# A filter with products of 128 columns, a re-ordered list, and the second gate/up tile in one piece

## The chip, the cores and the metric

One core of a Trainium2 chip runs the kernel. The metric is the device time of one execution in microseconds (us). The engines are TensorE (PE in the profile, with its weight loads apart as PEld), VectorE (DVE), ScalarE (ACT), GpSimd (POOL) and SyncE (SP, which issues most DMAs).

## The reference

Sequence S = 2048, width D = 512, hidden width F = 1376, all float32, one batch:

```python
def _A_ref(x, w_r, w_i):                      # spectral filter
    X = jnp.fft.rfft2(x, axes=(-2, -1))
    X = X * (w_r + 1j * w_i)                  # (2048, 257)
    return jnp.fft.irfft2(X, s=(S, D), axes=(-2, -1))

def _B_ref(x, w_gate, w_up, w_down):          # GEGLU
    h = _gelu(x @ w_gate) * (x @ w_up)        # tanh form of gelu
    return h @ w_down

h  = x + _A_ref(_layernorm(x), w_r, w_i)
h2 = h + _B_ref(_layernorm(h), w_gate, w_up, w_down)
```

## The kernel before

Both Fourier transforms are matmuls with cosine and sine tables. The kernel runs through these stages, each behind the other on TensorE:

- **START** (0 to 30 us): layer norm, and the transform over the sequence while x is loaded.
- **SECOND** (30 to 74 us), the filter, 16 blocks t of 128 rows of the spectrum. `over_d(t)` (step o; L423) transforms over D into two banks of PSUM, ScalarE copies them out as `dp` (L427, two copies of 64 partitions). `filtered(t)` (step f; L434) finishes the transform over the sequence from `dp`; DVE multiplies with the filter's weights `wt` (L440 to L442), and POOL adds the two products as `z` (L450, then L451, a correction of one column; for the last block DVE does this, with a part on POOL, L448). `back(t)` (step b; L461) begins the inverse. Step p patches two columns of `wt`, and each step h splits one piece of a gate or up weight into a high and a low part (ACT L156, POOL L157). `o` writes the banks that it names, in turn two pairs; a block's product therefore waits until ScalarE has copied out the block that had these banks before it.
- **FIRST** (74 to 119.5 us): the inverse over D (U, L527) and over the sequence (M, L866), the residual, the second layer norm, then, for pairs of row blocks, normalized blocks (R, ACT L909), their transposes (T, L560 and L566), and sums and differences of these, since gate, up and down are done by a scheme with 7 products in place of 8. Each operand is split into a high part (ACT) and a low part (DVE or POOL, L588), as each product is three float32r matmuls (`mm3`, L163 to L165). Steps a to o of a pair are these copies, sums and splits; K (POOL L827 to L830) prepares further row blocks; wl splits the down weights (POOL L508). The seven products P0 to P6 of the first gate/up tiles, g0 and g1, run between the steps, each tile in two halves a and b of 256 columns.
- Then tiles g2 and on, with the down products (L766), in a written order, 512 columns at a time, to the end, where `end` adds the last sums and stores them (L1211, L1216, L1217), the last block in two halves of 256 columns.

START, SECOND and FIRST are strings of step names. Inside them every engine runs its instructions in the order of the string, waiting in place for what an instruction needs. So the order of the work around the change is what these lists say: an engine can't pass an instruction of its own that waits.

In the filter one bank holds two parts of NQ/2 = 130 columns (even and odd frequencies; 129 and 128 are used, the rest are zeros of the tables). So L423 gives 4 products of 130 columns a block, `dp` has 520 columns and L434 gives 2 products of 260.

Of the kernel before, what the change touches and what calls it, by code (L numbers as in the profile page):

```python
# [19 lines left out]
S, D, F = 2048, 512, 1376  # L20
P = 128
# [3 lines left out]
NQ = 260  # L25
# [21 lines left out]
ROOTS = {0: 1, 1: 1, 2: 2, 4: 4, 8: 4, 12: 4}  # L47

FIRST = """
u0.1 u4.0 w4 C4.0 V4.2 X4 w0 C0.1 V0.3 X0 U1.2 C1.4 V1.0 X1 r0 U5.3 C5.5 V5.1 M4.1 O4.0 M0.2 O0.1 U2.3 H4 H0 X5 C2.5  # L50
V2.3 M5.1 H5 I4 G4 O5.0 G0 I0 S4 S0 A4 A0 E0.5 U7.2 C7.1 M1.3 O1.1 g0awh H1 Q0 N0 U6.0 C6.0 V7.4 X2 U3.4 C3.5 I5 G5 S5
M2.1 V6.3 R00 I1 G1 S1 A5 A1 R01 U9.7 C9 H2 X7 V3.1 X3 T00 a0 Q1 T01.2 s0.0 O2.1 U8.4 C8 E1.6 N1 R11 M7.0 c0 d0 f0
U12.3 e0.1 k0 R10 H7 b0 O7.0 g0 h0 C12 X6 M6.4 H6 i0 j0 T11.1 s1.2 r1 l0 T10 c1 d1 G2 I2 M3.2 O3.1 H3 G7 a1 b1 I7 S7
O6.0 U15.3 C15 e1.0 f1 g1 U14.5 C14 U10.4 C10 m0 k1 n1 g0aP0 g0ac1 g1aP0 l1 g0aP3 g0aP1 G3 I3 S3 A7 A3 Q3 g0aP2 I6 n0
G6 h1 g1ac1 E3.7 N3 g1aP2 i1 R31 T31.5 g1aP1 o1 R30 T30 S2 S6 A6 A2 g1ac2 j1 E2.6 Q2 N2 o0 g1aP4 g0awl s3.6 c3 g0ac2
g0aP4 R20 T20 a3 g1ac3 g1aP5 d3 e3.4 K9.5 m1 g0ad1 g0ac3 g0aP5 f3 b3 h3 g0ady g0aP6 i3 j3 R21 T21.7 g3 g1aP3 a2 b2
g0bP0 g0bP1 g1bP0 K12.4 g1ad1 g1ady g1aP6 r2 l3 k3 s2.8 g1aG0 c2 d2 f2 e2.7 k2 g1bP1 g1am0 g0bc1 g2 g0bP2 g1bc1 r3 n3
n2 o3 g1bP2 g0ad2 o2 g0aG0 g0am0 l2 m2 m3 g0bP3 h2 K8.4 g0aG1 g0am1 g0bc2 g0bP4 g1bd1 i2 j2 g1bc2 g1bP4 g1bG0 g1ad2
g0bc3 g0bd1 g0bdy g0ai0 g0ao0 g1aG1 g1bP3 g1ai0 g1am1 g1bc3 g1bdy g0ai1 g0ao1 g0bP6 g0bd2 g1awh g1awl g1ai1 g0bG1
g0bP5 hc g1bP6 lo1 lo2 g0bG0 g0bm0 g0bi0 g1bP5 g1bm0 g1bi0 g1bd2 g1bG1 g0bo0 U13.7 C13 lo3 g0bm1 g0bi1 U11.6 C11 g1bm1  # L60
g1bi1 g1ao0 g0bo1 g1bo0 g1bo1 g1ao1 g2P0
"""
# [57 lines left out]
def kernel(  # L120
# [48 lines left out]
    ps = ctx.enter_context(tc.tile_pool(name="ps", bufs=1, space=PSUM)).tile([P, 8, 512], F32, name="ps")  # L169
# [7 lines left out]
    k3 = ctx.enter_context(tc.tile_pool(name="k3", bufs=1))  # L177
# [57 lines left out]
    with (  # L235
# [146 lines left out]
        def keep_half(b):  # L382
            return dve.tensor_copy(*kept_of(b, slice(0, 2)))

        steps = {
            "s": stats,
            "g": merge,
            "m": mean,
# [21 lines left out]

        w1s.close()
        w2 = ctx2.enter_context(tc.tile_pool(name="w2", bufs=2, reuse_waits="tile"))
        dps, zs = {}, {}

        def over_d(t, k):

            pd = ps[:, k : k + 2]  # L420
            for c, (e, q) in enumerate(((0, 0), (1, 1), (0, 1), (1, 0))):
                o = pd[:, e, q * NQ // 2 : (q + 1) * NQ // 2]
                pe.matmul(o, ts[:, t, c].rearrange("p x b k -> p (x b k)"), dfs[:, c], start=True, stop=True)  # L423
            pdv = pd[:, :, :NQ].rearrange("p e (s q) -> p s e q", s=2)
            dps[t] = w2.tile([P, 2, 2, NQ // 2], F32, name="dp", bufs=5)
            for h, d in ((slice(0, 64), 1), (slice(64, P), -1)):
                act.activation(dps[t][h], pdv[h, ::d], AF.Copy)  # L427

        def filtered(t):
            dp, wt = dps.pop(t), wts.pop(t)  # L430
            px = ps[:, 4 + 2 * (t % 2) : 6 + 2 * (t % 2), :NQ]
            for g in range(2):
                r = dp[:, g].rearrange("p e q -> p (e q)")
                pe.matmul(px[:, g], cfs[:, min(t, 1), g], r, start=True, stop=True)  # L434
# [5 lines left out]
            dve.tensor_tensor(t1, px, wt[:, 0], op=ALU.mult)  # L440
# [9 lines left out]
            eng.tensor_tensor(z[:, :, first], t1[:, :, first], t2[:, :, first], op=ALU.add)  # L450
            eng.tensor_tensor(z[:, :, 0], z[:, :, 0], z[:, :, 128], op=ALU.add)  # L451
# [19 lines left out]
        with tc.manual_schedule(engines={et.PE, et.Activation, et.DVE, et.Pool}):  # L471
# [452 lines left out]
    def half(n, h):

        for k, f in tile_of(n, slice(2 * h, 2 * h + 2)).items():
            do[f"g{n}{'ab'[h]}{k}"] = f
        if not h:
# [62 lines left out]
    def second_half():  # L991
# [212 lines left out]
        def end(c, r, k, onto=False, halves=1, by=dve):  # L1204

            w = wds[NF - 1]
            for h in range(halves):
                cols = slice(h * 512 // halves, (h + 1) * 512 // halves)
                o = ps[:, k + h, : 512 // halves]
                for hw, ha in ((0, 0), (0, 1), (1, 0)):  # L1210
                    pe.matmul(o, w[:, hw, c * P : (c + 1) * P], last_a[:, ha, r, cols], start=not onto and hw + ha == 0, stop=hw == 1, skip_group_check=True)  # L1211
# [4 lines left out]
                by.tensor_tensor(to, o, to, op=ALU.add)  # L1216
                nc.sync.dma_start(ot[:, r, c, cols], to)  # L1217
# [89 lines left out]
def _tables():  # L1307
# [119 lines left out]
```

## Time and profile before

| what | value |
|---|---|
| time, median of 3 runs | 440.44 us (440.41 to 441.14) |
| the profiled execution | 440.5 us, its span 438.6 us |
| TensorE busy | 432.0 us, 98% of the span, 2275 matmuls recorded |
| DVE, ACT, POOL busy | 314.2, 243.1, 314.5 us |
| DMA | 41.61 MB, mean 95 GB/s |

In the tables of the profile a row of a timeline gives the start and the length in us (a run of like instructions is one row), the engine, the line, the operation, output <- inputs, the tiles' sizes and how often; brackets at the end give idle time of the engine just ahead and what ended it. A matmul of float32 is recorded as two. The length of a matmul row has its drain in it, so the pace of TensorE is read from the distance of starts.

### The profile page before, as it was taken

The page shows a single profiled execution, that of the slowest core. Times are in us where ns is not written, and L with a number is a line of the kernel's source. Part 1 is how long each engine was busy: PE and PEld are TensorE (multiplying, and loading weights), DVE is VectorE, ACT ScalarE, POOL GpSimd, SP SyncE. Part 2 cuts the span into 40 slices and gives each one's busy share as a digit, 9 for nine tenths or more (in the row PEclk, how much of TensorE's full clock was granted, in tenths as well). Part 3 has the DMA queues.
Part 4 walks back from the last instruction along what each step waited for, and adds up shares of the span by engine and source line. Part 5 has one row for each costly group of instructions (what it writes and reads, how often), then busy time and mean ns, then how long its engine had stood idle before and what let it go on. Part 6 is the DMA issues. An engine that isn't in the chain of part 4 may idle for free.

```text
span 438.6 us, 6625 instructions
## 1 busy us (share of the span) xinstructions
PE 432.0 (98%) x2275; PEld 366.8 (84%) x2275; DVE 314.2 (72%) x576; ACT 243.1 (55%) x502; POOL 314.5 (72%) x346
## 2 busy tenths in 40 slices
PE   8999999999999999999999999999999999999996
PEld 8999999789978777877888888888888888888885
DVE  5968896897864766368734579578677787687785
ACT  5989785799712442124432787376455653565640
POOL 6987796999859788648653944067879779787821
PEclk9999999999999999999999999999999999999999
DMA  8996904320023112112220203501212021200005
GB/s 284 400 411 85 380 10 156 128 73 24 25 96 97 49 53 92 48 50 72 72 73 24 72 25 120 169 11 62 73 48 72 28 69 49 72 24 2 0 2 192
DMA packets 23542, 41.61 MB, mean 95 GB/s; under 512 B 4178, under 2 KB 9810, under 8 KB 23380
## 3 DMA queue, kind: packets, MB, share of 16 engines
q1 hardware_dynamic: 23364, 41.05, 27.9%
q8 instruction: 18, 0.29, 0.3%
q10 hardware_dynamic: 144, 0.13, 0.1%
q14 instruction: 16, 0.13, 0.1%
HBM read 36.97 MB, written 4.20 MB: 94 GB/s over the span
## 4 chain that ended last, share of the span: by engine, by line
PE 80%; POOL 8%; DMA 5%; ACT 3%; issue 2%; DVE 1%; SPq 0%; DVEq 0%; POOLq 0%
PE ps L163 15%; PE ps L164 15%; PE ps L165 15%; PE ps L766 14%; PE ps L1105 11%; DMA gh<-in_x 3%; PE ps L527 3%; POOL z L450 3%; PE ps L866 2%; ACT dp L427 2%; DMA raw<-in_wgu 1%; PE ps L974 1%; POOL gu L157 1%; POOL pn L339 1%; PE ps L1211 1%
## 5 line engine op out<-in xcount | busy, mean ns | idle before, releaser
L163 PE MATMUL ps<-cb,gu 128*128 128x512 f32 (+1 forms) x336 | 127.2, 378 | 0.3 <-DVE a L692 0.3
L165 PE MATMUL ps<-cb,gu 128*128 128x512 f32 (+1 forms) x336 | 124.9, 372 | 0.0
L164 PE MATMUL ps<-cb,gu 128*128 128x512 f32 (+1 forms) x336 | 124.9, 372 | 0.0
L670 ACT ACTIVATE s<-ps 128x512 f32<-128x512 f32 (+1 forms) x72 | 40.4, 562 | 87.1 <-PE ps L165 86.7
L228 POOL TENSOR_TENSOR gu<-raw,gu 128x768 fp32r<-128x768 f32 (+1 forms) x42 | 61.3, 1481 | 29.0 <-DVE gu L223 16.7
L163 PEld LDWEIGHTS ps<-cb,gu 128*128 128x128 f32 x336 | 63.3, 188 | 12.3 <-issue 1.0
L164 PEld LDWEIGHTS ps<-cb,gu 128*128 128x128 f32 x336 | 63.3, 188 | 11.6 <-issue 1.0
L165 PEld LDWEIGHTS ps<-cb,gu 128*128 128x128 f32 x336 | 63.3, 188 | 11.1
L766 PE MATMUL ps<-wd,a 128*128 128x512 f32 x264 | 63.6, 393 | 0.0
L766 PEld LDWEIGHTS ps<-wd,a 128*128 128x128 f32 x264 | 49.1, 188 | 11.6 <-DVE gh L975 1.0
L679 DVE TENSOR_TENSOR ps<-ps,s 128x512 f32<-128x512 f32 (+1 forms) x48 | 31.1, 651 | 28.1 <-PE ps L165 25.3
L1112 DVE TENSOR_TENSOR gh<-ps,gh 128x512 f32<-128x512 f32 x66 | 44.2, 681 | 0.8 <-PE ps L1105 0.8
L676 ACT ACTIVATE s<-s 128x512 f32<-128x512 f32 (+1 forms) x48 | 28.4, 593 | 20.8 <-DVE s L673 20.7
L673 DVE TENSOR_TENSOR s<-ps,s 128x512 f32<-128x512 f32 (+1 forms) x48 | 30.7, 641 | 5.8 <-PE ps L165 4.7
L772 DVE TENSOR_TENSOR gh<-ps,gh 128x512 f32<-128x512 f32 x24 | 16.6, 690 | 25.3 <-PE ps L766 25.2
L508 POOL TENSOR_TENSOR wd<-wdr,wd 128x512 fp32r<-128x512 f32 x12 | 15.6, 1299 | 17.7 <-ACT wd L506 17.7
L673 DVE TENSOR_TENSOR ps<-ps,s 128x512 f32<-128x512 f32 (+1 forms) x24 | 15.7, 653 | 16.1 <-ACT s L670 15.6
L207 POOL TENSOR_TENSOR raw<-raw 128x256 f32<-128x256 f32 x16 | 11.9, 741 | 16.6 <-DMA raw<-in_wgu 14.9
L685 ACT ACTIVATE a<-ps 128x512 fp32r<-128x512 f32 (+1 forms) x26 | 13.8, 533 | 17.1 <-DVE ps L679 17.1
L1018 POOL TENSOR_TENSOR t<-mis,t 128x768 fp32r<-128x768 f32 (+1 forms) x9 | 13.3, 1481 | 13.2 <-ACT t L1016 13.2
L427 ACT ACTIVATE dp<-ps 64x520 f32<-64x520 f32 x32 | 19.1, 598 | 3.8 <-PE ps L423 3.3
L450 POOL TENSOR_TENSOR z<-t,t 128x520 f32<-128x520 f32 x15 | 19.4, 1296 | 1.0 <-DVE t L442 0.9
(182 smaller groups left out, 898.4 us busy)
## 6 DMA issues: line engine op xcount, KB each, us to landing
wt<-in_w SPq DMA_DIRECT2D x16, 520.0 KB, 7.7
raw<-in_wgu SPq DMA_DIRECT2D x32, 256.0 KB, 3.1
out<-gh SPq DMA_DIRECT2D x15, 256.0 KB, 2.0
gh<-in_x SPq DMA_DIRECT2D x7, 512.0 KB, 8.6
row<-in_x SPq DMA_DIRECT2D x12, 256.0 KB, 2.8
wdr<-in_wd SPq DMA_DIRECT2D x12, 256.0 KB, 2.6
mis<-in_wd SPq DMA_DIRECT2D x10, 256.0 KB, 2.6
a<-in_wgu SPq DMA_DIRECT2D x8, 256.0 KB, 3.1
```

What stands on the lines that cost most here:

```text
L163: pe.matmul(o, lh, rh, start=(i == 0 and not onto), stop=False, skip_group_check=True)
L164: pe.matmul(o, lh, rl, start=False, stop=False, skip_group_check=True)
L165: last = pe.matmul(o, ll, rh, start=False, stop=(i == n - 1), skip_group_check=True)
L228: pooled["lo"] = pool.tensor_tensor(r[:, 1, m], t[:, m], r[:, 0, m].bitcast(F32), op=ALU.subtract)
L450: eng.tensor_tensor(z[:, :, first], t1[:, :, first], t2[:, :, first], op=ALU.add)
L670: return lambda: act.activation(to, a, AF.Copy)
L673: return lambda: dve.tensor_tensor(to, a, b, op=ALU.add)
L676: return lambda: act.activation(g, g, AF.Gelu_apprx_tanh)
L679: return lambda: dve.tensor_tensor(u, u, g, op=ALU.mult)
L766: pe.matmul(o, parts_of[tiles.index((0, f))][:, ha, i // 4, r], wds[f][:, hw, c], start=start, stop=stop)
L1105: pe.matmul(ps[:, k], w[:, hw], a[ha], start=start and hw + ha == 0, stop=hw == 1, skip_group_check=True)
L1112: by.tensor_tensor(to, o, to, op=ALU.add)
```

## The change

1. The filter's products over D have 128 columns in place of 130 and L434 two pieces of 128 in place of 260. Frequency 256, which was column 128 of the even part, goes into column 0 of the sine table, which held zeros; the small table of weights for columns 0 and 256 is turned to match. The columns 128 and 129 of each part in PSUM, which DVE still reads, are cleared once, by a new step z4 on DVE ahead of the last copies of START. `dp` has 512 columns.
2. SECOND and FIRST are written in another order.
3. Tile g1 of gate and up is done whole, 512 columns at a time, as the tiles after it are (`part(1, slice(0, 4), "")`); g0 stays in halves.
4. The second half of the last store is issued by ScalarE's queue, not by SP's.

```diff
 START = """
-k8 f15 ... a14 b14 a15 b15 l15 k14 k15
+k8 f15 ... a14 b14 a15 b15 z4 l15 k14 k15
 FIRST = """
-u0.1 u4.0 w4 C4.0 V4.2 X4 w0 C0.1 V0.3 X0 U1.2 C1.4 V1.0 X1 r0 U5.3 C5.5 V5.1 M4.1 O4.0 M0.2 O0.1 U2.3 H4 H0 X5 C2.5
+u4.0 u0.1 w4 C4.0 V4.2 X4 w0 C0.1 V0.3 U1.2 X0 C1.4 V1.0 X1 U5.3 C5.5 V5.1 M4.1 O4.0 H4 r0 M0.2 O0.1 U2.3 X5 M5.1 G4
...
 SECOND = """
-h p0 h o0.6 o1.0 h o2.2 p1 h f0 o3.0 f1 p2 o4.2 f2 o5.0 p3 h f3 o6.2 p4 o7.0 h h p5 f4 p6 o8.2 p7 p8 f5 b0 b1 f6 h h
+h p0 o0.6 o1.0 h h o2.2 h p1 f0 f1 p2 o3.0 o4.2 h f2 o5.0 h p3 p4 f3 o6.2 o7.0 h f4 o8.2 p5 f5 p6 p7 b0 o9.2 f6 p8 p9
...
-        dfs = cp.tile([P, 4, NQ // 2], F32, name="dfs")
+        dfs = cp.tile([P, 4, P], F32, name="dfs")
+        def clear(k):
+            dve.memset(ps[:, k:, :NQ].rearrange("p k (e q) -> p k e q", e=2)[:, :, :, P:], 0.0)
-                o = pd[:, e, q * NQ // 2 : (q + 1) * NQ // 2]
+                o = pd[:, e, q * NQ // 2 :][:, :P]
                 pe.matmul(o, ts[:, t, c].rearrange("p x b k -> p (x b k)"), dfs[:, c], start=True, stop=True)
-            pdv = pd[:, :, :NQ].rearrange("p e (s q) -> p s e q", s=2)
-            dps[t] = w2.tile([P, 2, 2, NQ // 2], F32, name="dp", bufs=5)
+            pdv = pd[:, :, :NQ].rearrange("p e (s q) -> p s e q", s=2)[:, :, :, :P]
+            dps[t] = w2.tile([P, 2, 2, P], F32, name="dp", bufs=5)
-                pe.matmul(px[:, g], cfs[:, min(t, 1), g], r, start=True, stop=True)
+                o = px[:, g].rearrange("p (e q) -> p e q", e=2)[:, :, :P]
+                pe.matmul(o, cfs[:, min(t, 1), g], r, start=True, stop=True)
-    for n in range(2):
-        for h in range(2):
-            half(n, h)
+    part(0, slice(0, 2), "a")
+    part(0, slice(2, 4), "b")
+    part(1, slice(0, 4), "")
-                nc.sync.dma_start(ot[:, r, c, cols], to)
+                (nc.scalar if h else nc.sync).dma_start(ot[:, r, c, cols], to)
-    df[:, 2, 1:129] = np.sin(ae[:, 1:])
+    df[:, 2, 1:128], df[:, 2, 0] = np.sin(ae[:, 1:128]), np.sin(ae[:, 128])
-    we = np.stack([np.stack([a[m][..., [0, 256]] for a in (A_w_r, A_w_i)], 3) for m in (k, -k % S)])
+    we = np.stack([np.stack([a[m][..., [256, 0]] for a in (A_w_r, A_w_i)], 3) for m in (k, -k % S)])
```

What the lists move, at three places. First TensorE in the filter's middle, from step f4 on. Before:

```order
L434 MATMUL ps<-dp,cfs 128x260 x2
L423 MATMUL ps<-dfs,ts 128x130 x4
L434 MATMUL ps<-dp,cfs 128x260 x2
L461 MATMUL ps<-cis,z 128x2x64 x8
L434 MATMUL ps<-dp,cfs 128x260 x2
L423 MATMUL ps<-dfs,ts 128x130 x4
```

These are f4, o8, f5, b0 with b1, f6, o9. Now:

```order
L436 MATMUL ps<-dp,cfs 128x2x128 x2
L424 MATMUL ps<-dfs,ts 128x128 x4
L436 MATMUL ps<-dp,cfs 128x2x128 x2
L463 MATMUL ps<-cis,z 128x2x64 x4
L424 MATMUL ps<-dfs,ts 128x128 x4
L436 MATMUL ps<-dp,cfs 128x2x128 x2
```

Here o9 stands ahead of f6 and b1, with f5 and b0 alone between it and o8, whose banks it takes.

Second, GpSimd in the last third of the filter: z is a block's sum, gu a weight's low part, raw a sum of pieces of the weights that are loaded. Before:

```order
L451 TENSOR_TENSOR z<-z 128x2
L157 TENSOR_TENSOR gu<-raw,gu 128x256
L450 TENSOR_TENSOR z<-t_752,t_753 128x520
L451 TENSOR_TENSOR z<-z 128x2
L450 TENSOR_TENSOR z<-t_775,t_776 128x520
```

The splits stand there one at a time between the sums. Now:

```order
L214 TENSOR_TENSOR raw<-raw 128x256
L156 TENSOR_TENSOR gu<-raw,gu 128x256
L452 TENSOR_TENSOR z<-t_740,t_741 128x520
L453 TENSOR_TENSOR z<-z 128x2
L156 TENSOR_TENSOR gu<-raw,gu 128x256 x4
L452 TENSOR_TENSOR z<-t_785,t_786 128x520
```

Four splits stand together ahead of the sum of block 12.

Third, GpSimd ahead of "m1", the low part (into cb, from s3) that product P6 of tile g0 needs; wd is the down weights, gh and row are K's row block. Before:

```order
L588 TENSOR_TENSOR cb_892<-s1_917,cb_892 128x2x128
L588 TENSOR_TENSOR cb_892<-s2_918,cb_892 128x2x128
L508 TENSOR_TENSOR wd_990<-wdr_988,wd_990 128x512
L827 TENSOR_TENSOR row_901<-gh_58 128x2x128
L828 TENSOR_TENSOR row_901<-gh_58 128x2x128
L829 TENSOR_TENSOR gh_58<-row_901 128x256
L830 TENSOR_TENSOR gh_58<-row_901 128x256
L588 TENSOR_TENSOR cb_892<-s3_919,cb_892 128x2x128
```

Now:

```order
L590 TENSOR_TENSOR cb_893<-s1_918,cb_893 128x2x128
L829 TENSOR_TENSOR row_901<-gh_58 128x2x128
L830 TENSOR_TENSOR row_901<-gh_58 128x2x128
L831 TENSOR_TENSOR gh_58<-row_901 128x256
L832 TENSOR_TENSOR gh_58<-row_901 128x256
L590 TENSOR_TENSOR cb_893<-s3_920,cb_893 128x2x128
```

One K stays ahead of m1, the split of the down weights (L508) has gone behind it. On TensorE 18 matmuls of tile g0's first half (L163 to L165) stand ahead of the transposes of pair 3, where there were 36 of g0 and g1; the steps U11 and U13 remain the last ahead of g2. From g2 on the two programs have the same order.

More of the change, by code (lines that the diff above doesn't have):

```diff
@@ L37 @@
 c11 k4 a7 b7 f12 f14 q13 s15 v8 g12 s14 k3 b6 k7 g15 a8 a9 k5 g14 r12 v10 n12 b8 v12 b9 k9 c12 a11 u13 c13 a10 b10 u14
-k8 f15 b11 a12 b12 k6 a13 k10 c14 c15 k11 v14 u15 b13 k13 k12 v15 a14 b14 a15 b15 l15 k14 k15
+k8 f15 b11 a12 b12 k6 a13 k10 c14 c15 k11 v14 u15 b13 k13 k12 v15 a14 b14 a15 b15 z4 l15 k14 k15
 """
@@ L49 @@
 FIRST = """
-u0.1 u4.0 w4 C4.0 V4.2 X4 w0 C0.1 V0.3 X0 U1.2 C1.4 V1.0 X1 r0 U5.3 C5.5 V5.1 M4.1 O4.0 M0.2 O0.1 U2.3 H4 H0 X5 C2.5
[L51 to L59, printed above, removed]
@@ L60 @@
-g0bP5 hc g1bP6 lo1 lo2 g0bG0 g0bm0 g0bi0 g1bP5 g1bm0 g1bi0 g1bd2 g1bG1 g0bo0 U13.7 C13 lo3 g0bm1 g0bi1 U11.6 C11 g1bm1
-g1bi1 g1ao0 g0bo1 g1bo0 g1bo1 g1ao1 g2P0
+u4.0 u0.1 w4 C4.0 V4.2 X4 w0 C0.1 V0.3 U1.2 X0 C1.4 V1.0 X1 U5.3 C5.5 V5.1 M4.1 O4.0 H4 r0 M0.2 O0.1 U2.3 X5 M5.1 G4
+I4 H0 I0 G0 C2.5 V2.3 H5 S4 A4 O5.0 G5 S0 A0 U7.2 C7.1 I5 g0awh E0.5 M1.3 O1.1 X2 Q0 U6.0 C6.0 H1 G1 I1 N0 R01 U3.4
+R00 U9.7 M2.1 V7.4 T01.2 X7 S5 V6.3 X6 C3.5 T00 O2.1 s0.0 S1 A1 A5 V3.1 X3 U8.4 C9 H2 G2 c0 E1.6 d0 Q1 N1 C8 M7.0 H7
@@ new lines @@
+U12.3 e0.1 f0 g0 k0 a0 b0 h0 O7.0 l0 M6.4 H6 M3.2 R11 T11.1 R10 I2 O3.1 n0 H3 I7 G7 O6.0 S7 s1.2 T10 c1 i0 j0 U10.4
+C12 l1 a1 U14.5 U15.3 d1 e1.0 m0 G3 I3 S3 A7 G6 A3 I6 f1 k1 o0 b1 g0aP0 E3.7 Q3 C14 g1 g0aP1 n1 N3 S6 r1 g0ac1 g0aP2
+h1 S2 A6 o1 R31 T31.5 R30 T30 K12.4 i1 A2 m1 K9.5 g0ac2 g0awl Q2 j1 g0ad1 E2.6 g0aP4 N2 s3.6 c3 d3 g0aP3 R20 T20 g0ac3
+g0ady g0aP6 g0aP5 a3 b3 r2 e3.4 h3 a2 b2 g0bP1 l3 i3 R21 j3 T21.7 g0aG0 g0am0 C15 f3 k3 g3 s2.8 c2 d2 C10 l2 g0bP0
+g0bc1 f2 g2 g0ad2 g1P0 g1c1 n3 e2.7 k2 n2 m2 h2 i2 j2 g1P1 o2 g1d1 g0bP2 g0bc2 g1wh g1P2 g1c2 g0bP3 g0bd1 o3 g0bP4
@@ L62 @@
+g0aG1 g0am1 g1P4 m3 g0bc3 g0bdy g0bP6 g0bd2 r3 g1G0 g0ai1 g0ao1 g1c3 K8.4 g0bP5 hc g0bG0 g0bm0 g0bi0 g1P3 g1P5 g1dy
+g1P6 g0ai0 g1wl g0bG1 g0bm1 g0bi1 g1m0 g1i0 g0bo0 g1d2 g1G1 U11.6 C11 U13.7 C13 lo1 lo2 lo3 g0ao0 g2P0 g0bo1 g1m1 g1o0
+g1i1 g1o1
 """
 SECOND = """
-h p0 h o0.6 o1.0 h o2.2 p1 h f0 o3.0 f1 p2 o4.2 f2 o5.0 p3 h f3 o6.2 p4 o7.0 h h p5 f4 p6 o8.2 p7 p8 f5 b0 b1 f6 h h
-o9.2 p9 h h p10 b2 f7 o10.2 f8 b3 o11.2 b4 p11 h h h f9 o12.2 p12 f10 h p13 b5 f11 o13.2 b6 p14 f12 p15 o14.2 h b7 f13
@@ L67 @@
-h o15.2 f14 b8 b9 f15 b10 b11 h b12 b13 b14 b15
+h p0 o0.6 o1.0 h h o2.2 h p1 f0 f1 p2 o3.0 o4.2 h f2 o5.0 h p3 p4 f3 o6.2 o7.0 h f4 o8.2 p5 f5 p6 p7 b0 o9.2 f6 p8 p9
+b1 f7 o10.2 h p10 f8 h b2 o11.2 f9 b3 o12.2 h f10 h h b4 p11 f11 p12 p13 o13.2 b5 b6 o14.2 p14 h h h h f12 f13 o15.2
+b7 b8 p15 f14 b9 h f15 b10 h b11 b12 b13 b14 b15 h
 """
@@ L383, in keep_half @@
             return dve.tensor_copy(*kept_of(b, slice(0, 2)))
+        def clear(k):
+            dve.memset(ps[:, k:, :NQ].rearrange("p k (e q) -> p k e q", e=2)[:, :, :, P:], 0.0)
         steps = {
+            "z": clear,
             "s": stats,
@@ L922, in pair, with part @@
             do[f"{k}{i}"] = lambda z, k=k: ops[k](places[z])
[L924 to L928, printed above, removed]
+    def part(n, i, mark):
+        for k, f in tile_of(n, i).items():
+            do[f"g{n}{mark}{k}"] = f
+        if mark != "b":
             down = load_d(tiles[n][1])
-            do[f"g{n}awh"] = do[f"g{n}awl"] = lambda: next(down)
+            do[f"g{n}{mark}wh"] = do[f"g{n}{mark}wl"] = lambda: next(down)
     for b in range(8):
@@ L1325, in _tables @@
     ae, ao = 2 * np.pi / D * d[:, None] * qe, 2 * np.pi / D * d[:, None] * qo
-    df = np.zeros((P, 4, NQ // 2))
+    df = np.zeros((P, 4, P))
     df[:, 0, 1:128] = np.cos(ae[:, 1:128])
     df[:, 1, :128] = np.sin(ao)
-    df[:, 2, 1:129] = np.sin(ae[:, 1:])
+    df[:, 2, 1:128], df[:, 2, 0] = np.sin(ae[:, 1:128]), np.sin(ae[:, 128])
     df[:, 3, :128] = np.cos(ao)
```

## The prediction

> **What bounds the kernel now.** I read the page first, then the busy time in three stretches, then the timelines of single engines round the places that the change touches. From the page, the clock row (tenths of full speed in 40 slices) and the chain of work that ended last:
>
> ```profile
> PEclk9999999999999999999999999999999999999999
> PE 80%; POOL 8%; DMA 5%; ACT 3%; issue 2%; DVE 1%; SPq 0%; DVEq 0%; POOLq 0%
> ```
>
> The clock is full throughout, and four fifths of the chain is TensorE's own work. The stretches below are the filter (30.20 to 74.04 us), the inverse with the first gate and up products (to 119.51) and all later tiles; columns: length, then busy time and instructions of PE, weight load, DVE, ACT and POOL, clock, DMA share, GB/s.
>
> ```profile
> 30.20:74.04 43.84, 43.52 (x320) 40.96 (x320) 36.01 (x51) 35.61 (x80) 37.13 (x52) 1.00 0.54 167
> 74.04:119.51 45.47, 45.20 (x345) 41.05 (x345) 37.46 (x95) 37.34 (x92) 40.96 (x57) 1.00 0.23 76
> 119.51:434.20 314.69, 314.64 (x1388) 257.31 (x1389) 216.56 (x368) 146.46 (x269) 211.71 (x211) 1.00 0.19 61
> ```
>
> PE lacks 0.32 us in the first, 0.27 in the second, 0.05 in the third. So re-ordering can win at most about 0.6 us, and beyond that only less TensorE work or a shorter tail helps. It can lose much more: in the second stretch POOL is busy 40.96 of 45.47 us, in the first DVE, ACT and POOL each 35.6 to 37.1 of 43.84, so an order that asks a result of them earlier finds no slack.
>
> **The change part by part: TensorE's work.** Starts of consecutive groups in the filter give each product's pace:
>
> ```profile
> 58.05 1.06 PE L423 MATMUL ps<-dfs,ts 128*128 128x130 f32 x8
> 58.94 1.05 PE L461 MATMUL ps<-cis,z 128*128 128x128 f32 x8
> 59.83 1.04 PE L434 MATMUL ps<-dp,cfs 128*128 128x260 f32 x4
> 60.71 1.06 PE L423 MATMUL ps<-dfs,ts 128*128 128x130 f32 x8
> ```
>
> Eight records of 130 columns take 0.89 us, eight of 128 also 0.89 (L461): cutting L423 from 130 to 128 columns gains nothing that shows, at most 2/130 of its 16 x 0.89, so 0.2 us. Four records of 260 take 0.88; at the same cost per column, 256 saves 4/260 of it, 0.0135 us, in each of 16 steps: −0.2 us. The new output is two pieces of 128 columns with two left out between; L461 already writes two separate pieces of 64 and keeps L423's pace, so I put the gap at nothing. The Trainium skill, page "PSUM — Partial Sum Buffer", section "Specifications (TRN2)", says that any non-contiguous access to PSUM slows matmuls significantly. By that rule the filter would grow by several us instead of shrinking; the equal paces of L461 and L423 above speak against it here.
>
> Tile 1 of gate and up: the pace of 256-column and of 512-column products is
>
> ```profile
> 95.52 0.28 PE L164 MATMUL ps<-cb,gu 128*128 128x256 f32 x1
> 95.64 0.28 PE L165 MATMUL ps<-cb,gu 128*128 128x256 f32 x1
> ...
> 293.79 0.39 PE L164 MATMUL ps<-cb,gu 128*128 128x512 f32 x1
> 295.38 0.39 PE L165 MATMUL ps<-cb,gu 128*128 128x512 f32 x1
> ```
>
> 0.12 us, and 1.59 us for seven of 512 columns (the two rows lie seven starts apart in one unbroken run), 0.227 each. 7 products of 6 instructions in two halves are 84 x 0.12 = 10.08 us; whole they are 42 x 0.227 = 9.53: −0.55. Less TensorE work in all: −0.75.
>
> **The new clear on DVE** (16 numbers a partition) goes ahead of the last copy of the start:
>
> ```profile
> 29.67 0.42 DVE L383 COPY ts<-ps 128x256 f32<-128x256 f32 x1 [0.65 <-PE ps L372]
> ```
>
> DVE was idle 0.65 us there, which hides it: 0. If its place in the queue costs as long as a 128x2 addition on DVE (0.73, below), up to 0.25 of it shows.
>
> **The filter's order.** The tenth product over D (t = 9, L423, "o9") now comes after f5 and b0 instead of after f6 and b1. It writes the banks out of which ScalarE copies dp of t = 8.
>
> ```profile
> 30.20 2.92 PE L423 MATMUL ps<-dfs,ts 128*128 128x130 f32 x24 [0.19 <-issue]
> 44.22 1.21 ACT L427 ACTIVATE dp<-ps 64x520 f32<-64x520 f32 x2
> 46.51 0.72 PE L423 MATMUL ps<-dfs,ts 128*128 128x130 f32 x5
> ```
>
> ScalarE is through with that copy at 45.43, and nothing in its queue ahead of it becomes notably shorter (one weight split goes behind the first copy, none leaves). PE's work ahead of o9 is nine products over D, six filters, one back: 9 x 0.89 + 6 x 0.865 + 0.89 = 14.1, so it is there at 44.3 and waits about 1.1 us (before it came at 46.51, without a wait). After o9's start come 7 x 0.89 + 10 x 0.865 + 9 x 0.89 = 22.9 until the last filter step, f15, ends at 68.3. What then follows:
>
> ```profile
> 66.93 1.04 PE L434 MATMUL ps<-dp,cfs 128*128 128x260 f32 x4
> ...
> 71.92 2.05 PE L461 MATMUL ps<-cis,z 128*128 128x128 f32 x16 [0.25 <-POOL z L451]
> 74.04 1.16 PE L527 MATMUL ps<-dis,gh 128*128 128x128 f32 x8
> ```
>
> ```profile
> 66.20 0.70 DVE L440 TENSOR_TENSOR t<-ps,wt 128x520 f32<-128x520 f32 x1
> ...
> 70.51 1.30 DVE L450 TENSOR_TENSOR z<-t,t 128x260 f32<-128x260 f32 x1
> 71.84 0.73 DVE L451 TENSOR_TENSOR z<-z 128x2 f32<-128x2 f32 x1
> ```
>
> DVE's t14 and t15 take 4.31 us together (66.20 to 70.51), sum and correction 2.06. f14 ends one back and one filter step before f15, at 66.6; then 66.6 + 4.3 + 2.06 = 72.95 for the last z. Before, the same point was 72.57, and the last back step began at 72.81, behind one that had waited for POOL. That wait goes (no weight split stands ahead of POOL's last additions now), DVE's chain takes its place. The next stage begins at about 74.3 instead of 74.04: +0.3. Bounds: −0.5, if o9 hardly waits, and +0.6, if the four weight splits that now stand together in POOL's queue delay z12 to z14.
>
> **The inverse and the first products.** The list now asks for tile 0's last products sooner: the transposes of the third pair come after 18 products of tile 0 rather than 36 of tiles 0 and 1. POOL makes the low halves of their operands:
>
> ```profile
> 99.05 1.30 POOL L508 TENSOR_TENSOR wd<-wdr,wd 128x512 fp32r<-128x512 f32 x1
> 100.30 0.75 POOL L827 TENSOR_TENSOR row<-gh 128x256 f32<-128x256 f32 x1
> ...
> 102.54 0.74 POOL L830 TENSOR_TENSOR gh<-row 128x256 f32<-128x256 f32 x1
> 103.24 0.74 POOL L588 TENSOR_TENSOR cb<-s,cb 128x256 fp32r<-128x256 f32 x1
> ```
>
> ```profile
> 99.72 0.60 PE L566 MATMUL ps<-ident,a 128*128 128x128 f32 x4
> ...
> 104.62 0.28 PE L163 MATMUL ps<-cb,gu 128*128 128x256 f32 x1
> ...
> 117.29 1.95 PE L527 MATMUL ps<-dis,gh 128*128 128x128 f32 x16
> 119.51 0.50 PE L163 MATMUL ps<-cb,gu 128*128 128x512 f32 x1 [0.27 <-DVE a L692]
> ```
>
> The split at 103.24 ("m1") ends at 103.98, and the product that needs it ("g0aP6") began at 104.62, on time. In the new POOL order the same work stands ahead of m1 but for the 1.30 of the down weights: it ends at 102.7. A shift of the stage by 0.3 disappears on the way: POOL waited at
>
> ```profile
> 80.17 2.79 POOL L880 TENSOR_TENSOR gh<-a,t 128x256 f32<-128x256 f32 x4 [0.32 <-DVE a L876]
> ```
>
> for a load, not for PE. PE without waits would be at g0aP6's second matmul at 100.4 (the list's matmuls ahead of it at these paces, from 74.3). So it waits 2.3 us in all, spread over the third pair's transposes, the split before ("o1") and m1. Even without m1 the transposes of pair 2 hold it: they need a normalized block that ScalarE had at
>
> ```profile
> 101.13 0.73 ACT L909 ACTIVATE a<-gh,rs 128x512 f32<-128x512 f32 x1
> ```
>
> 101.86, and would have 1.0 to 1.4 sooner. From g0aP6's second matmul to the third tile's first product PE has 53 matmuls of 256 columns (6.36), 42 of 512 (9.53), four transposes (0.44) and 16 records of L527 (2 x 0.89 at the pace above, 1.78): 18.1. So that product starts at 102.75 + 18.1 + 0.1 = 120.95, not 119.51: **+1.4**. This holds the −0.75 and the filter's +0.3 already. Bounds: 118.3 with no wait at all (119.51 less 0.27, 0.75 and some ramp, with the filter as before) and 121.8, if a further split comes late.
>
> After it the program is the old one, and PE has no idle time to give or take (0.05 in 314.69).
>
> **The last store.** DVE's last addition ends at 435.19; SP issues two stores, 0.44 each, the second behind the first:
>
> ```profile
> 433.84 1.35 DVE L1216 TENSOR_TENSOR gh<-ps,gh 128x512 f32<-128x512 f32 x3 [0.67 <-PE ps L1211]
> 434.99 0.88 SPq L1217 DMA_DIRECT2D out<-gh  x2
> ```
>
> The second began at 435.43, 0.24 after its data. ScalarE has nothing left then and can begin at 435.2: **−0.2** (0 to −0.24; if its issue took twice as long, +0.2). Nothing is queued behind it.
>
> Sum: 1.4 − 0.2 = about +1.15 on the profiled execution's 440.5 us (span 438.6), so 441.65; that execution lies 0.06 above the median, 440.44, so **441.6**. A measurement of this kernel can tell about 0.2%, 0.88 us, from no change.
>
> **The rivals.** (1) *PE is not held* (faster, 0.10): POOL's order brings each split in time, g2's first product comes at 118.3, −1.2, and the store gives −0.2: 439.1. For it speaks that the work falls by 0.75; against it, POOL's 40.96 busy us of 45.47: even closely packed, m1 isn't done by 100.4. (2) *Work saved pays the waits* (no change, 0.27): o9 waits half as long, the filter gains 0.3, POOL runs without its idle time and m1 ends 0.6 sooner; g2 starts at 120.3, +0.8 − 0.2: 441.1, or less. (3) *A second late split* (slower, 0.15): the half-tile products of tile 0's second half follow the fourth pair's transposes by under 4 us, while DVE and POOL make their sums; if one comes 0.9 late, PE waits again: 442.5. It decides once a split of the fourth pair ends after about 108 us. (4) *The clock falls in the new idle time* (slower, 0.02). At the start the page's clock is not seen low, yet the first records are slow:
>
> ```profile
> 1.37 5.38 PE L174 MATMUL ps<-ident 128*128 128x128 f32 x28 [1.37 <-POOL ident masks.py:199]
> ```
>
> 0.19 us each, against 0.11 later: 28 such records again would cost 2.2 us, so 443.8. It needs a gap like the first one; I expect none above 1.3 us. The Trainium skill, page "TensorE: Matmul & The Clock Gate", summarises that idle gaps beyond about 3 us put the array back to half rate; by that rule too the gaps forecast here don't do it. (5) *The change doesn't do what it says* (slower, 0.01): the output with a gap runs at half pace, 64 x 0.22 = +14 us, 455.
>
> **How the numbers follow.** My forecast has 0.45; its own range is 441.0 to 442.4. Faster by over 0.2% is rival 1: 0.10. Within it is rival 2: 0.27. Slower is the forecast with rivals 3, 4 and 5: 0.63. The range 440.2 to 442.8 leaves out rival 1, 4 and 5 and the ends of 2 and 3, under 0.2 together.
>
> **What would show it.** Right: L434's four records at 0.865; a PE wait of about 1 us before an L423 group near 44.3, released by ACT; the last back step behind DVE's correction (L453 there); PE idle 2 to 2.5 us between 95 and 104 in several pieces, the last one released by POOL's L590 (the old L588); g2's first product near 121 with no DVE wait ahead of it; a store on ScalarE's queue near 435.2 plus the shift. Wrong: no PE idle time over 0.5 us in 74 to 120 (rival 1), idle time after 104 (rival 3), or a stretch of slow records (rivals 4 and 5).

## The result, and the profile after

| | before | changed |
|---|---|---|
| time, median of 6 runs | 440.79 us (440.11 to 441.42) | 444.50 us (444.39 to 444.61) |
| the profiled execution, its span | 440.5, 438.6 us | 444.61, 442.7 us |

The changed kernel is slower, ratio 1.0075 (95% interval 1.0062 to 1.0089): 3.7 us between the medians, 4.1 between the profiled executions. The forecast was slower, but by 1.15 us, and 444.5 lies outside its range of 440.2 to 442.8.

From the page after, the clock and the chain that ended last:

```profile
PEclk9999999999999999999999999999999999999999
PE 88%; ACT 5%; DVE 2%; DMA 2%; issue 1%; SPq 0%; DVEq 0%; ACTq 0%
```

The clock did not fall in the profiled execution. POOL, 8% of the chain before, is gone from it. Two stretches of the kernel after, with the columns of the tables by stretch above:

```profile
30.20:74.04 43.84, 43.84 (x320) 40.85 (x320) 34.97 (x51) 35.32 (x80) 37.23 (x52) 1.00 0.55 167
124.00:438.00 314.00, 313.95 (x1387) 256.90 (x1386) 215.42 (x364) 146.12 (x267) 208.67 (x210) 1.00 0.19 61
```

TensorE is filled in the filter and from 124 us on. So the loss lies between. The next two answers list TensorE's waits from 74 to 124 us by the engine that ended them, of before and then of after (total us, times, longest):

```profile
PE ps L163 <- DVE a L692: 0.3, 1, 0.3
```

```profile
PE ps L162 <- DVE ps L681: 1.3, 1, 1.3
PE ps L868 <- DVE cb L590: 0.4, 1, 0.4
PE ps L562 <- ACT a L911: 0.3, 1, 0.3
PE ps L529 <- DVE cb L590: 0.3, 1, 0.3
PE ps L162 <- DVE ps L675: 0.3, 1, 0.3
PE ps L529 <- ACT t L873: 0.2, 1, 0.2
```

One wait has become six, and 0.3 us has become 2.8; none is POOL's. Where TensorE stands, from its timeline after:

```profile
74.24 0.94 PE L529 MATMUL ps<-dis,gh 128*128 128x128 f32 x6
...
105.58 0.60 PE L568 MATMUL ps<-ident,a 128*128 128x128 f32 x4
107.51 0.39 PE L162 MATMUL ps<-cb,gu 128*128 128x256 f32 x1 [1.33 <-DVE ps L681]
...
120.62 0.50 PE L162 MATMUL ps<-cb,gu 128*128 128x512 f32 x1 [0.30 <-DVE ps L675]
...
123.81 0.48 PE L162 MATMUL ps<-cb,gu 128*128 128x512 f32 x1
```

The last transposes before, and the product behind them:

```profile
105.34 0.60 PE L566 MATMUL ps<-ident,a 128*128 128x128 f32 x4
105.69 0.36 PE L163 MATMUL ps<-cb,gu 128*128 128x256 f32 x1
```

The inverse begins at 74.24 (74.04 before), the last transposes stand at 105.58 (105.34 before), and the third tile begins at 123.81 (119.51 before). Up to the last transposes the two kernels are 0.24 us apart, but they have not done the same work. Tile products up to there, before and after, one of the three lines each:

```profile
L165 PE MATMUL ps<-cb,gu 128*128 128x256 f32 x24 | 6.8, 284 | 0.0
```

```profile
L164 PE MATMUL ps<-cb,gu 128*128 128x256 f32 x16 | 4.5, 282 | 0.0
```

Before, 72 matmuls of tiles 0 and 1 were done; now 48, all of tile 0. At 0.12 us the 24 are 2.9 us of work; since the whole tile 1 takes 0.55 less, 2.3 us more work is left behind the transposes. A wait costs more than its own length, since TensorE stops and starts again: from the transposes to the next product are 1.93 us after (105.58 to 107.51) and 0.35 before, 1.58 more, of which 1.33 are recorded as a wait and 0.25 are the restart. With the 0.24, with the waits of 1.33 and 0.30 behind the transposes and 0.25 for each, less the one wait of 0.27 with its 0.25 that before has there, this makes 4.2 of the 4.3 us. The four other waits, 1.2 us in all, lie ahead of the transposes; with their restarts they are about 2 of the 2.6 us that TensorE lost there (2.9 less 0.24).

The long wait is followed back in ScalarE's and DVE's timelines after:

```profile
104.55 0.71 ACT L911 ACTIVATE a<-gh,rs 128x512 f32<-128x512 f32 x1
105.28 1.28 ACT L678 ACT_TABLE_LOAD   x1
106.58 0.42 ACT L678 ACTIVATE s<-s 128x256 f32<-128x256 f32 x1
```

```profile
107.03 0.43 DVE L681 TENSOR_TENSOR ps<-ps,s 128x256 f32<-128x256 f32 x1 [1.87 <-ACT s L678]
```

The new list has g0aG0 and g0am0 (tile 0's first gelu, and DVE's product with it) ahead of g0bP0. That matmul writes the bank of PSUM in which DVE's product stands, so it waits for DVE, DVE for the gelu, and the gelu for the load of its table. Before, the same load had work of TensorE beside it:

```profile
106.64 1.28 ACT L676 ACT_TABLE_LOAD   x1
```

The Trainium skill, page "ScalarE: Activation LUTs", section "What ACT_TABLE_LOAD costs", gives about 1283 ns for the load and about 1380 ns for a drain on top. The load's 1.28 us agrees; a drain isn't seen here, since the row ahead ends 0.02 us before the load and the gelu begins 0.02 behind it.

### The profile page after: what moved, and what is told of

The parts are those of the page before. It is cut to its first block, busy times and chain, and to the rows that moved or that the text cites. A ratio compares the mean times of both kernels' runs of the same rounds, so it can differ in the third digit from the quotient of the medians.

```text
span 442.7 us, 6530 instructions
## 1 busy us (share of the span) xinstructions
PE 433.6 (98%) x2233; PEld 364.4 (82%) x2233; DVE 313.0 (71%) x570; ACT 242.8 (55%) x495; POOL 314.6 (71%) x346
## 4 chain that ended last, share of the span: by engine, by line
PE 88%; ACT 5%; DVE 2%; DMA 2%; issue 1%; SPq 0%; DVEq 0%; ACTq 0%
PE ps L162 16%; PE ps L163 15%; PE ps L164 15%; PE ps L768 14%; PE ps L1107 11%; PE ps L424 3%; PE ps L436 3%; PE ps L463 3%; PE ps L529 3%; DMA gh<-in_x 2%; PE ps L976 1%; ACT ts L379 1%; PE ps L1213 1%; PE ps L868 1%; ACT ms L329 1%
## 5 line engine op out<-in xcount | busy, mean ns | idle before, releaser
L162 PE MATMUL ps<-cb,gu 128*128 128x512 f32 (+1 forms) x322 | 124.8, 388 | 1.7 <-DVE ps L681 1.3
L163 PE MATMUL ps<-cb,gu 128*128 128x512 f32 (+1 forms) x322 | 122.6, 381 | 0.0
L164 PE MATMUL ps<-cb,gu 128*128 128x512 f32 (+1 forms) x322 | 122.4, 380 | 0.0
L162 PEld LDWEIGHTS ps<-cb,gu 128*128 128x128 f32 x322 | 60.5, 188 | 14.9 <-DVE ps L681 1.6
L163 PEld LDWEIGHTS ps<-cb,gu 128*128 128x128 f32 x322 | 60.5, 188 | 12.4 <-issue 1.0
L164 PEld LDWEIGHTS ps<-cb,gu 128*128 128x128 f32 x322 | 60.5, 188 | 11.6
L428 ACT ACTIVATE dp<-ps 64x512 f32<-64x512 f32 x32 | 19.0, 593 | 4.0 <-PE ps L424 3.6
```

The lines of the kernel that those rows point to most:

```text
L162: pe.matmul(o, lh, rh, start=(i == 0 and not onto), stop=False, skip_group_check=True)
L163: pe.matmul(o, lh, rl, start=False, stop=False, skip_group_check=True)
L164: last = pe.matmul(o, ll, rh, start=False, stop=(i == n - 1), skip_group_check=True)
```

## The experiments

The changed kernel again (e5) had 444.71 us (444.32 to 444.99), so times of changed kernels compare between chips within some 0.2 us. The kernel before scattered more on later chips (440.4 to 443.5), so ratios to it are less sharp there.

**The old FIRST (e1, and e15 again).** Edit: FIRST as before, with tile 1 in halves; the rest is the changed kernel.

```diff
-FIRST = """u4.0 u0.1 w4 C4.0 V4.2 X4 ...
+FIRST = """u0.1 u4.0 w4 C4.0 V4.2 X4 ...
-    part(0, slice(0, 2), "a")
-    part(0, slice(2, 4), "b")
-    part(1, slice(0, 4), "")
+    for n in range(2):
+        for h in range(2):
+            half(n, h)
```

> The changed kernel with the old FIRST and so with tile 1 in halves; narrow products, new SECOND and the store on ScalarE stay. Theory (the loss lies in FIRST: its order has TensorE wait 4 us between 90 and 121 us): 440.8 to 441.2 us, that is within 0.4 of before, third tile's first product near 119.6 in the profile. Rival (the filter's shape or order loses too, and later stages only show it): above 442.5 us.

> The kernel of the first experiment again, for comparisons on one chip: 440.8 us, 0.1 to 0.3% below before.

Measured 440.78 us (440.60 to 441.09), ratio to before 0.9979 (0.9967 to 0.9991), and 440.87, ratio 0.9979 (0.9969 to 0.9989). So all of the loss is FIRST with the whole tile, and the other parts together win about 0.2% by the medians: this is the fastest version run. The win is that the longer executions are missing; the shortest ones of the kernel before on the same chips (440.61 and 440.42) are as fast as those of e1 and e15 (440.60 and 440.55).

**The gelu behind g0bP0 (e2).**

```diff
-... T21.7 g0aG0 g0am0 C15 f3 k3 g3 s2.8 c2 d2 C10 l2 g0bP0 g0bc1
+... T21.7 C15 f3 k3 g3 s2.8 c2 d2 C10 l2 g0bP0 g0aG0 g0am0 g0bc1
```

> The changed kernel with the steps g0aG0 and g0am0 (gelu of tile 0's first half, and the product with it on DVE) behind g0bP0 in FIRST. Theory (g0bP0 waits for DVE's product in the same bank of PSUM, this for the gelu, and this for ScalarE's table load of 1.28 us): the wait of 1.33 us ahead of g0bP0 goes, 443.0 to 443.3 us. Rival (the next product that needs ScalarE's copy behind the table load, or a late split, waits in its place): 444.1 us or more.

Measured 444.79 us (444.37 to 445.97). The rival held. The timeline of TensorE in it:

```profile
110.73 0.39 PE L162 MATMUL ps<-cb,gu 128*128 128x256 f32 x1 [1.17 <-ACT cb L587]
111.45 0.38 PE L163 MATMUL ps<-cb,gu 128*128 128x256 f32 x1 [0.34 <-DVE cb L590]
```

The wait ahead of g0bP0 is gone, and 1.5 us of waiting stands three products later, where ScalarE's copies, now behind the table load, are late. So the loss does not hang on the gelu's place alone. The profiled execution was the slowest, 445.97; the last section shows what happened in it.

**No table load there (e3).**

```diff
+    do["g0aG0"] = lambda: act.activation(sums[0][0][:, : 2 * P], sums[0][0][:, : 2 * P], AF.Copy)
```

> The changed kernel with a plain copy in place of the one gelu g0aG0 (the gelu of tile 0's first half is left out), so that the table load moves to the next gelu, some 7 us later. Theory (the table load is what makes g0bP0 late): the wait falls from 1.33 us to 0.1 or less, 443.1 to 443.4 us. Rival (DVE's queue or the gelu's place make it late, not the load): 444.2 us or more.

A plain copy stands in place of this half's gelu, which is left out. Measured 443.56 us (443.40 to 443.67), 1.1 below e5. The wait ahead of g0bP0 is gone, and the next gelu, with the load, brings one of 0.6 us:

```profile
115.30 0.38 PE L162 MATMUL ps<-cb,gu 128*128 128x256 f32 x1 [0.60 <-DVE ps L675]
```

So moving the load to the next gelu gains about 1.1 of the 3.8 us that lie between the changed kernel and e1. The load is still there and costs this wait; a kernel without any load was not measured.

**The load earlier (e6, e10).**

```diff
-... E2.6 g0aP4 N2 s3.6 c3 ...
+... E2.6 g0aP4 N2 s3.6 table c3 ...
e6:
+    early_to = w3.tile([P, 1], F32, name="early", bufs=1)
+    do["table"] = lambda: act.activation(early_to, eps, AF.Gelu_apprx_tanh)
e10:
+    dve.memset(eps_all[:, :3], EPS)
+    do["table"] = lambda: act.activation(eps_all[:, 1:2], eps_all[:, 2:3], AF.Gelu_apprx_tanh)
```

> The changed kernel with a gelu of one column into a scratch tile behind step s3 in FIRST, so that ScalarE loads its table there, at about 100.9 us, where it idles 0.6 us, and not at 105.3. Theory (the load's 1.28 us has no cover at its place; wherever it stands on ScalarE's queue in this stretch only the idle time there hides it): the normalized block behind it comes 0.7 us late, the wait ahead of g0bP0 goes: 443.9 us. Rival (the load is fully hidden there): 443.2. Rival (the transposes' wait grows by all that is won): 444.5.

> The early table load once more, its gelu now into a spare column of a tile that exists already, so that no buffer of the kernel moves. The first one was 0.4 us ahead of the changed kernel at 130 us and lost 3.1 us after it, with the down products at 236 ns instead of 230. Theory (the lost time came from buffers 4 bytes off their places, not from the load): 444.1 to 444.4 us, down products at 230 ns. Rival (the load's place does it): 447.

The step "table" is a gelu of one column, which e6 writes into a new tile and e10 into a spare column of an old one. Measured 447.06 us (446.97 to 447.16), then 443.96 (443.84 to 444.74). In e10 the transposes wait:

```profile
103.00 0.66 PE L563 MATMUL ps<-ident,a 128*128 128x128 f32 x4 [1.10 <-ACT a L912]
```

1.10 us instead of 0.33, and g0bP0 not at all. So some 0.75 us is won by the medians, less than half of what the wait cost with its restart; two of e10's five executions (444.57 and 444.74) show nothing of it. e6 and e10 are 3.1 us apart and differ in where this column lies (last section).

**The old head (e9).** FIRST in the old order as far as g0aP0, in the new one from there.

```diff
-... U14.5 U15.3 d1 e1.0 m0 G3 I3 S3 A7 G6 A3 I6 f1 k1 o0 b1 g0aP0 E3.7 Q3 C14 g1 g0aP1 ...
+... U15.3 C15 e1.0 f1 g1 U14.5 C14 U10.4 C10 m0 k1 n1 n0 l1 G3 I3 S3 A7 G6 A3 I6 o0 g0aP0 E3.7 Q3 g0aP1 ...
```

> The changed kernel with FIRST in the old order up to the first product of tile 0 (g0aP0), and in the new order from there, steps done already left out. Theory (the three waits of 0.5 us at 90.6, 93.3 and 94.7 us come from the new head, which asks for banks of PSUM earlier than DVE and ScalarE give them back; the later waits are the tail's own): 443.2 to 443.6 us. Rival (POOL and ScalarE set the pace behind, and what the head wins is waited for again at the transposes): 444.2 to 444.7.

Measured 444.48 us (444.25 to 444.94): the rival. TensorE's waits from 74 to 124 us in it:

```profile
PE ps L152 <- DVE ps L671: 1.3, 1, 1.3
PE ps L152 <- ACT s L662: 0.7, 1, 0.7
PE ps L552 <- ACT a L901: 0.3, 1, 0.3
```

The three waits at 91 to 95 us are gone, a new one of 0.7 us stands at 97.8, and those of 0.3 and 1.3 have stayed. TensorE was 1.5 us ahead at 95 us and no longer at 100. What it must wait for here is made by the other engines at their own pace, and a TensorE that comes sooner waits longer.

**Cover taken from the old order (e13).**

```diff
-... g0aP0 g0ac1 g1aP0 l1 ... g1ac1 ... g1aP2 ... g1aP1 ... g1ac2 ... g1aP4 ... g1ac3 g1aP5 ... T21.7 g3
+... g0aP0 g0ac1 l1 ... T21.7 g3 g1aP0 g1ac1 g1aP2 g1aP1 g1ac2 g1aP4 g1ac3 g1aP5
```

> The kernel of the first experiment (old FIRST, tile 1 in halves: 440.8 us) with the eight steps of tile 1's first half that stand ahead of the last transposes (five products, 30 matmuls, 3.6 us of TensorE's work, and three copies) moved behind these, to where the sums of pair 3 are done. Theory (the new order loses because TensorE has none of tile 1's work left to do while DVE, ScalarE and POOL make the last two pairs' operands): TensorE waits 2 to 3.6 us ahead of the last transposes and ends that much later, 442.8 to 444.4 us. Rival (the new order loses by its order on DVE and ScalarE, not by the cover): 441.5 us or less.

Cover is work that TensorE has at hand while the other engines make its next operands. Measured 445.12 us (445.00 to 445.38) against 440.87 for e15 on the same chip: 4.25 us lost, more than the whole change loses. TensorE's waits from 74 to 124 us in it:

```profile
PE ps L152 <- ACT s L662: 1.9, 4, 0.5
PE ps L558 <- ACT a L901: 0.6, 1, 0.6
```

e15 has one wait of 0.3 there. The last transposes, in e15 and then in e13:

```profile
105.38 0.60 PE L569 MATMUL ps<-ident,a 128*128 128x128 f32 x4
```

```profile
104.77 0.60 PE L558 MATMUL ps<-ident,a 128*128 128x128 f32 x4
```

With 30 matmuls, 3.6 us, fewer ahead of them TensorE came there only 0.61 us sooner: the other engines set this time, and the rest was spent waiting. Nothing but the place of tile 1's five early products and their three copies differs, so the lack of cover alone can cost what the change costs. That it also costs it in the new order is argued from the count of 72 against 48 and from the transposes at 105.58 there; the new order with tile 1's early half put back was not run.

**Ready work into the wait (e14).**

```diff
-... T21.7 g0aG0 ... g1G1 U11.6 C11 U13.7 C13
+... T21.7 U13.6 g0aG0 ... g1G1 C13 U11.7 C11
```

U13 takes a bank that sums of pair 2 still read, so these aren't the reference's in it.

> The changed kernel with the inverse over D of one late row block (U13, 0.89 us of TensorE's work that depends on nothing in this stretch) from the end of FIRST to the place behind the last transposes, where TensorE waits 1.33 us for the gelu. Theory (what lacks there is work that is ready): the wait shrinks by 0.89, 443.6 to 443.9 us. Rival (the wait comes back at the next step that DVE or ScalarE has to finish, as it did in the second experiment): 444.4 or more.

Measured 444.19 us (444.02 to 444.46), 0.5 below e5. The wait ahead of g0bP0 is 0.44 instead of 1.33, as forecast; 0.4 us of the 0.89 is lost again later (a wait of 0.22 stands ahead of the third tile). Half of the theory's gain: inconclusive by its own bounds (443.6 to 443.9, or 444.4).

**Tile 1 in halves in the new order (e8).** Each step of g1 becomes one for half a and one for half b.

```diff
-g1P0 g1c1 ...
+g1aP0 g1bP0 g1ac1 g1bc1 ...
```

In this order the first product of half b, a new start in the same bank, comes while half a still adds up there, and tile 1's values differ from the reference's; that the one makes the other was not tested.

> The changed kernel, its order kept, with tile 1 in two halves, each step of it as one for half a and one for half b in the same place. The prediction's size: the 42 more matmuls add 0.55 us, 445.0 us. Rival (its DVE and ScalarE steps, now twice as many, are late): 446 us or more. Rival (finer steps let DVE and ScalarE begin sooner and take off the waits of tile 1): 444.5 or less.

Measured 444.95 us (444.79 to 445.07), 0.24 above e5 on the same chip, with ranges that overlap. So the whole tile's saving, 0.55 by the count, shows here as some 0.2 if at all, and going back to halves in this order does not undo the loss; what the whole tile costs is the place at which its products can begin.

**Narrow products alone (e7).**

```diff
-dfs ... NQ // 2, dp ... NQ // 2, output 260 in one piece
+dfs ... P, dp ... P, output 2 x 128, z4 in START; lists and stores as before
```

> The kernel before with the narrow products alone (128 columns, z4, the tables): old SECOND, old FIRST, tile 1 in halves, SyncE's store. The prediction's sizes: 0.2 us less than before (4 columns of 260 in 64 records, at the same pace a column). Rival (two pieces with a gap cost pace): slower than before by 1 us or more. Rival (nothing, since the last blocks' DVE chain sets the stage's end): within 0.1.

Measured 441.36 us (440.30 to 442.56), ratio 0.9985 (0.9973 to 0.9998). Not slower: the output with a gap costs nothing that shows. The size, 0.2 us, is within the interval.

**The store on SyncE (e4).**

```diff
-(nc.scalar if h else nc.sync).dma_start(ot[:, r, c, cols], to)
+nc.sync.dma_start(ot[:, r, c, cols], to)
```

> The changed kernel with the second half of the last store on SyncE's queue again. The prediction's step: 0.2 us slower than the changed kernel, 444.7. Rival, by the trace (the span ends 3.4 us behind DVE's last addition in both kernels): no difference, 444.5.

Measured 444.69 us (444.65 to 444.77), against 444.71 (444.32 to 444.99) for e5: no difference. The last two stores before, and the last one after, in the tables of DMA issues (the last number: us from issue to landing):

```profile
out<-gh SPq DMA_DIRECT2D x2, 128.0 KB, 2.0
```

```profile
out<-gh ACTq DMA_DIRECT2D x1, 128.0 KB, 2.2
```

ScalarE's issue begins 0.23 us sooner behind DVE's last addition, and the store lands 0.2 us later after its issue.

**Two attempts that failed (e11, e12).**

```diff
-g0bP6 g0bd2 r3 ... g0bP5 hc g0bG0
+g0bP6 r3 hc g0bd2 ... g0bP5 g0bG0                     # e11, on the changed kernel
-g0bi0 g1bP5 g1bm0 g1bi0 g1bd2 g1bG1 g0bo0
+g0bi0 g1bP5 g0bo0 g1bm0 g1bi0 g1bd2 g1bG1             # e12, on e1
```

> The changed kernel with DVE's cast of the next weights (step hc, 2.07 us) ahead of the sum g0bd2, where DVE idles 1.25 us, and not ahead of the step that g1P6 waits for. Theory (this wait at 120 us, 0.4 us, is DVE's queue): it goes, 444.1 us. Rival (what hangs on g0bd2 is late instead): 444.5 or more.

> Narrow products, new SECOND and the store on ScalarE with the old FIRST, as in the first experiment, and in it g0bo0 (the last reader of the bank that the third tile's first product takes) ahead of g1bm0, g1bd2 and g1bG1. Theory (the 0.26 us ahead of that product is DVE's queue): 440.5 us, 0.2 to 0.3 below the first experiment and some 0.9 below before. Rival (DVE waits for ScalarE's copy instead, the old wait stays): 440.8.

e11: 447.18 us. The cast writes into a buffer of weights that g0bP5 still reads, so that product isn't the reference's here, and TensorE waits 1.65 us for the cast. e12: 441.39 us (441.30 to 441.50), 0.6 above e1; the wait of 0.26 became 0.16, and one of 0.67 appeared a product later, also behind DVE. Both only moved a wait along DVE's queue.

## Why the prediction was wrong, step by step

- **Paces: right.** In the filter after, four records of 256 columns take 0.86 us and eight of 128 take 0.89:

```profile
65.79 1.03 PE L436 MATMUL ps<-dp,cfs 128*128 128x256 f32 x4
66.65 1.05 PE L463 MATMUL ps<-cis,z 128*128 128x128 f32 x8
67.54 1.03 PE L436 MATMUL ps<-dp,cfs 128*128 128x256 f32 x4
```

The gap in the output costs no pace. What the Trainium skill, page "PSUM — Partial Sum Buffer", section "Specifications (TRN2)", says of non-contiguous access is not borne out for two pieces of 128 columns.
- **The filter's order: right in sum (74.24, forecast 74.3), not in its terms.** o9 began at 45.18 and hardly waited, since TensorE had waited for ScalarE's copies, 0.1 to 0.2 a time, at the products over D ahead of it (each of these, and o9 too, began 0.05 us behind the end of a copy). DVE's last sum and correction took 1.07 us, not 2.06, and TensorE's last back steps did not wait for them. That the errors cancel is luck:

```profile
71.33 0.49 DVE L452 TENSOR_TENSOR z<-t,t 128x260 f32<-128x260 f32 x1
71.86 0.58 DVE L453 TENSOR_TENSOR z<-z 128x2 f32<-128x2 f32 x1
```

- **m1: the time nearly right, the reason not.** POOL ended it at 103.21 (forecast 102.7), and g0aP6's second matmul began at 103.27 (forecast 102.75):

```profile
102.48 0.73 POOL L590 TENSOR_TENSOR cb<-s,cb 128x256 fp32r<-128x256 f32 x1
...
103.27 0.38 PE L163 MATMUL ps<-cb,gu 128*128 128x256 f32 x1
```

But the last piece of the forecast wait of 2.3 us was to end on POOL, and none did. TensorE came to g0aP6 only at 103.01, held up by DVE and ScalarE at 91 to 95 us and by ScalarE's normalized block just ahead:

```profile
101.49 0.72 ACT L911 ACTIVATE a<-gh,rs 128x512 f32<-128x512 f32 x1 [0.61 <-DVE rs L907]
102.27 0.66 PE L562 MATMUL ps<-ident,a 128*128 128x128 f32 x4 [0.33 <-ACT a L911]
```

This block was forecast 1.0 to 1.4 us sooner than 101.86 and was done at 102.21, as ScalarE waited for DVE's scale. m1 itself held TensorE by some 0.06 us (0.26 from g0aP6's first matmul to its second; 0.20 from 103.10 to 103.30 behind the same transposes before). That both came together near 103 is luck.
- **The step that failed: "From g0aP6's second matmul to the third tile's first product ... 18.1".** The prediction added TensorE's work there as if nothing waited. It took 20.5, so 2.4 of the 2.9 us by which the third tile came late (123.81, forecast 120.95) lie here, and 0.5 at m1. The wait of 1.33 ahead of g0bP0 and of 0.30 ahead of g1P6 were missing; with 0.25 for each restart they make 2.1 of the 2.4. The prediction read order and waits of POOL, which had been the chain's second engine, and did not follow the matmuls behind m1 back to DVE and ScalarE; the table load, hidden in the trace of before, was not priced at all. Where it says that the third pair's transposes come after 18 products rather than 36, it spent this only on the waits ahead of m1, though the work that is missing there also bares the waits behind.
- **Rival 3, a second late wait, was the right kind with the wrong place and under half the price.** It named the fourth pair's splits behind 108 us; the waits were at 107.5 and 120.6, behind a gelu and a sum in DVE's queue, 2.1 us with the restarts instead of 0.9.
- **The store: mis-sized.** −0.2 forecast, 0 measured: what ScalarE's earlier issue gains, its later landing takes.
- What the new order costs beyond e10, e3 and the lost cover was not taken apart further. e9 and e2 show that single moves in it only shift the wait. Whether some order of these steps makes the whole tile win was not settled.

## What to carry to other kernels

Ask of a step that is merged into a larger one when its earliest part could run before: half of tile 1 was TensorE's cover while the other engines made the last operands, and 0.55 us of saved work cost 2.9 us of cover. Follow each matmul behind the moved place back through all engines that release it, hidden table loads and same-bank writers too, and not only through the engine that led the chain. A wait that goes when one step is moved, and comes back three products later, says that the supply is late, not the place.

## What was not expected of the hardware

**A new tile of 4 bytes a partition, and slower matmuls.** e6 and e10 differ in the scratch tile, and in two more columns of one memset. The down products from 140 to 430 us in e6, then in e10 (count, busy us, mean ns):

```profile
L768 PE MATMUL ps<-wd,a 128*128 128x512 f32 x232 | 57.2, 398 | 0.0
```

```profile
L769 PE MATMUL ps<-wd,a 128*128 128x512 f32 x230 | 55.3, 392 | 0.0
```

By distance of starts, where nothing idles, these are 233 against 227 ns, and the gate and up products about 1 ns slower; over the whole kernel e6 takes 3.1 us more, not much less than the change itself. e11, as slow (447.18) without a new tile, has its down products at 227. That e6's tile moved later buffers, and that this is the cause, is inferred from the difference between the two; the buffers' addresses are not known.

**The clock fell behind 1.5 us of waiting.** Stretches of e2's profiled execution (granted clock: the number after POOL's):

```profile
108.00:112.00 4.00, 2.49 (x12) 1.67 (x12) 1.61 (x4) 3.49 (x8) 2.06 (x3) 1.00 0.25 66
112.00:113.00 1.00, 1.00 (x7) 0.87 (x6) 0.55 (x2) 0.81 (x4) 0.80 (x2) 0.92 0.00 0
113.00:114.00 1.00, 1.00 (x4) 0.81 (x3) 1.00 (x3) 0.49 (x1) 1.00 (x2) 0.50 0.00 0
114.00:115.00 1.00, 1.00 (x6) 0.91 (x6) 0.08 (x1) 0.65 (x2) 1.00 (x3) 0.50 0.00 0
115.00:116.00 1.00, 1.00 (x6) 1.00 (x6) 0.43 (x1) 0.26 (x1) 1.00 (x2) 0.50 0.00 0
116.00:117.00 1.00, 1.00 (x8) 0.90 (x7) 0.00 (x0) 0.31 (x2) 0.92 (x2) 0.87 0.00 0
```

After waits of 1.17 and 0.34 us within 1 us the clock was halved for some 3.5 us, which fits that this execution was the slowest of the five. Three of the other four were 1.2 to 1.6 us faster, so the same list of steps does not always meet a low clock. In the changed kernel's profiled execution, with its single wait of 1.33 us, the clock stayed full. The Trainium skill, page "TensorE: Matmul & The Clock Gate", section "Why this matters for your kernels", speaks of gaps beyond about 3 us; here it fell behind shorter ones that lay close together.

**With the new SECOND the time is steadier.** Before, DVE waited in the filter for a load:

```profile
54.87 0.70 DVE L440 TENSOR_TENSOR t<-ps,wt 128x520 f32<-128x520 f32 x1 [1.05 <-DMA wt<-in_w]
```

After, it doesn't. Kernels with the old SECOND scattered by 1.3 to 2.7 us (e7: 440.30 to 442.56; before beside e13: 440.42 to 443.14), those with the new one by 0.1 to 0.9 (e1: 440.60 to 441.09; e15: 440.55 to 441.11), but for e2 with its 1.6. That the load's time makes the scatter was not tested by itself.
